# Three paired attention steps and one seven-product set in a fused attention and MLP kernel

## The chip, the core and the metric

The kernel runs on one core of one Trainium2 chip. Its engines are TensorE (PE, matmuls; PEld is its weight load), VectorE (DVE), ScalarE (ACT), GpSimd (POOL) and SyncE (SP, which here only issues DMAs; its queue is SPq). The metric is the device time of one execution in microseconds, the median of several runs.

## The reference, cut to what matters

```
for b in range(12):                       # blocks of 64 tokens, 4 batches x 8 heads, head_dim 64
    intra = einsum(qb, kb) * Dmask        # Dmask[i, j] = lam ** (i - j) for j <= i
    intra = einsum(intra, vb)
    inter = einsum(qb * lam_pow, kv_state)
    out[block] = intra + inter
    kv_state = lam_block * kv_state + einsum(kb * rev_pow, vb)
x = out as 3072 tokens x 512
h = x @ w_in                              # 512 x 2048: "first dense product"
result = gelu_tanh(h) @ w_out             # 2048 x 512: "second dense product"
```

All inputs and the result are float32; the kernel computes its products from float16 copies.

## The kernel before

**Steps.** The 3072 tokens are 12 superblocks of 256 tokens. A superblock has two halves of the heads, so there are 24 attention steps, numbered 0 to 23: step n is superblock n // 2, heads of half n % 2. A step loads q, k and v (`load_step`, line 70), casts and scales them (`prep_qk`: q on DVE at line 271, k on ACT at line 276; `prep_v`: v on POOL at line 258), and turns q and k around with a transposing DMA from step 9 on (line 280). `prep_v(s)` also issues the loads of step s + 3. Then come score matmuls of 64x64 blocks (`scores`, line 327), the causal mask on DVE into `PT` (`causal`, line 337, two instructions for a step), state products K (line 362), PT times v (line 376), and products with the carried state (line 385). `update` carries the state: t on DVE (lines 478 and 481), then u on POOL (line 488). ACT copies the step's output into `xT` (`x_out`, line 462). The first superblock of a batch has no carried state in its first half block, and the last one of a batch makes no state for a next.

**Two forms of a step.** `R(n, s)` runs the scores of step n and the outputs of the step s = n - 1. `burst(ns, ss)` does two steps of each at once, in whole classes: all scores, all PT products (line 411), all K products (line 425), all state products (line 436), then the masks. A burst holds four score banks, two O banks and two K banks of the eight PSUM banks of the pool `psM`, which every other matmul uses too. Before the change steps 8 to 17 go by `R` in the loop over `FILL`, and 18 to 23 by bursts.

**Dense products.** The tokens go through the dense products in seven groups: `groups = [[0, 1], [2], [3], [4, 5], [6, 7], [8, 9], [10, 11]]`. Group g becomes available when its last superblock's output is computed; `queue_group(g)` then appends its pieces to the list `filler`, and `fill(n)` runs the next n pieces between the parts of the attention steps. TensorE runs instructions in the order in which they are written, so the places of `fill` in the program are the schedule. In groups 3 and 4 (512 tokens) the first dense product is 16 pieces `mm1` of four matmuls of 128x512 (line 529), each followed by a gelu on ACT (line 533); the second is seven block products (`product`, line 606) in place of eight, with sums of blocks made on DVE (`sum_g`, line 576). Groups 5 and 6 (`SEVEN`) do the first product by seven block products as well: `seven(m, k)` (line 698) for m of 1 to 7 and sets k of 0 to 3, each four matmuls of 128x256. The sums of blocks of x are made by `sum_x` (line 677), those of w_in by `sum_win` (line 151). In a set, products 1, 6, 7 and 4 accumulate in one bank X one after the other: m1 is copied out by ACT (line 709), X after m6 is copied out by DVE (line 711), X after m7 is added to q by DVE (line 719), X after m4 goes through the gelu (line 715). 5 and then 3 share a bank Y, and 2 has a bank W. In groups 5 and 6 other pieces lie between these, and the sets alternate between two X banks.

**Buffers that the change touches.** Each transposing DMA writes one of four `qkT` buffers (pool `qkp`), which is free once the last product of its step has read it. The converted q, k and v have five buffers each, `PT` three, `u` four for each half. Every DMA in this part is issued by SP, in program order.

Of the kernel before, what the change touches and what calls it, by code (L numbers as in the profile page):

```python
# [9 lines left out]
FP16 = mybir.dt.float16  # L10
AF = mybir.ActivationFunctionType
ALU = mybir.AluOpType
# [3 lines left out]
def kernel(  # L16
# [10 lines left out]
    nc = tc.nc  # L27
    pin = tc.keep_in_program_order
    P = 128
    B, H, S, D = q.shape  # L30
    SB = 256
    NSB = S // SB
    HH = H // 2
# [136 lines left out]
    def load_ahead(s):  # L170
        if s < NSTEP:
            load_step(s)
# [72 lines left out]
    def prep(s):  # L245
        prep_qk(s)
        prep_v(s)

    def wide(t):
        return t.rearrange("p j h d -> p h j d")  # L250

    def decay(t, s):
        hs = halves[s % 2]
        return t[:, hs, :].unsqueeze(3).to_broadcast([P, HH, 2, D])

    def prep_v(s):
        tv = a16p.tile([P, 2, HH, D], FP16, tag="v16", name=f"v16_{s}")
        pin(nc.gpsimd.tensor_tensor(wide(tv[:]), ld32[s][2][:], decay(dv, s), ALU.mult))  # L258
        a16[s] = a16[s] + (tv,)
        if s >= 6:  # L260
            if s + 3 == FIRST_DMA_T + 1:
                load_step(s + 3, "qk")
            else:
                load_ahead(s + 3)

    def prep_qk(s):
        q32, k32, _ = ld32[s]
        tqk = a16p.tile([P, 2, 2, HH, D], FP16, tag="qk16", name=f"qk16_{s}")
        tq, tk = tqk[:, 0], tqk[:, 1]
        q_eng = nc.gpsimd if s == 3 else nc.vector  # L270
        pin(q_eng.tensor_tensor(wide(tq), q32[:], decay(dq, s), ALU.mult))  # L271
        if s == 0:
            inverse(halves[0])
            odd(halves[1])
            inverse(halves[1])
        pin(nc.scalar.activation(out=wide(tk), in_=k32[:], func=AF.Copy))  # L276
        a16[s] = (tq, tk)
        if s >= FIRST_DMA_T:
            o = qkp.tile([P, 2, 2, 2, P], FP16, tag="qkT", name=f"qkT_{s}")
            pin(nc.sync.dma_start_transpose(out=o[:].rearrange("p a j h t -> p (a j h) t"),  # L280
                                            in_=tqk[:].rearrange("p a j h d -> p (a j h d)")))
            qkT[s] = o
            if s == FIRST_DMA_T:
                load_step(s + 1, "v")
# [107 lines left out]
    def burst(ns, ss, *mix):  # L392


        for n in ns:
            scores(n)
        O = [ps_M.tile([P, 2, 2, P], FP32, tag="M", name=f"O{c}") for c in range(2)]
        seen = set()

        def start(kind, c, hl):  # L400
            new = (kind, c, hl) not in seen
            seen.add((kind, c, hl))
            return new

        qTs = [qkT.pop(s) for s in ss]
        for i, s in enumerate(ss):
            PT, tv = PTs.pop(s), a16.pop(s)[2]
            for hp in range(2):
                for jk in range(2):
                    for c, hl in TILES:  # L410
                        pin(nc.tensor.matmul(
                            O[c][half64(hl), i, hp, :], tv[half64(c), jk, 2 * hp + hl, :],
                            PT[half64(c), hl, hp, jk, :], start=start("O", c, hl), stop=False,
                            skip_group_check=True))
        if ns:
            K = [ps_M.tile([P, 2, P], FP32, tag="M", name=f"K{c}") for c in range(2)]
        for i, n in enumerate(ns):
            _, tk, tv = a16[n]
            last = (n // 2) % NSB == NSB - 1
            for jk in range(2):  # L420
                for hp in range(2):
                    for c, hl in TILES:
                        if c == 1 and last:
                            continue
                        pin(nc.tensor.matmul(
                            K[c][half64(hl), i, hp * D : hp * D + D],
                            tk[half64(c), jk, 2 * hp + hl, :], tv[half64(c), jk, 2 * hp + hl, :],
                            start=start("K", c, hl), stop=(jk == 1), skip_group_check=True))
            Kps[n] = [t[:, i] for t in K]
        for i, s in enumerate(ss):  # L430
            for c in range(2):
                if c == 0 and (s // 2) % NSB == 0:
                    continue
                u = us.pop((s, 0) if c else (s - 2, 1))
                for hp in range(2):
                    pin(nc.tensor.matmul(O[c][:, i, hp, :], u[:, hp].rearrange("p l d -> p (l d)"),
                                         qTs[i][:, 0, :, hp, half64(c)], start=False, stop=True,
                                         skip_group_check=True))
        for n in ns:
            causal(n)  # L440
        for i, s in enumerate(ss):
            x_out(s, [t[:, i].rearrange("p h t -> p (h t)") for t in O])
        sbg = ss[-1] // 2
        g, i = group_of[sbg]
        if i == len(groups[g]) - 1:
            queue_group(g, *mix)
        for n in ns:
            update(n, 0)
# [55 lines left out]
        return gs_kept[1:]  # L504

    SEVEN = (5, 6)
    SLOTS = {5: {1: 0, 2: 1, 5: 1, 6: 1, 3: 1, 7: 1}, 4: {1: 0, 2: 1, 5: 0, 6: 1, 3: 1, 7: 1}}
    groups = [[0, 1], [2], [3], [4, 5], [6, 7], [8, 9], [10, 11]]
    group_of = {sb: (g, i) for g, sbs in enumerate(groups) for i, sb in enumerate(sbs)}
# [2 lines left out]
    def queue_group(g, lead=0, per_set=0):  # L512
# [69 lines left out]
        def product(m, p, part=None):  # L582
# [42 lines left out]
            def store(T, ps=slice(0, NP), es=slice(0, 2)):  # L625
                r = row0 + T * HN
                rows = out[r : r + HN, :].rearrange("(p q) (e d) -> q p e d", q=P, e=2)
                whole = g == 3 or (g, T) == (4, 0)
                for i in [ps] if whole else [slice(i, i + 1) for i in range(ps.start, ps.stop)]:
                    pin(nc.sync.dma_start(out=rows[:, i, es], in_=out_tile(T)[:, i, es, :]))  # L630

# [53 lines left out]
        def seven(m, k):  # L685
# [48 lines left out]
                added(1, 1, "q")  # L734
            elif m == 4:
                pending.insert(0, lambda: gelu(1, 0, dst[:]))
            if k == HF // 2 - 1 and m in (3, 7, 4):
                release()

        def merge(lead, per_set):  # L740
# [71 lines left out]
        def behind(k, i0, i1, ms):  # L812

            piece = filler[at + k]

            def both():
                piece()
                sum_g(i0, i1, ms)

            filler[at + k] = both  # L820
# [3 lines left out]
        if g in SEVEN:  # L824
# [6 lines left out]
            for k, m in enumerate((2, 4, 3)):  # L831
                behind(len(parts) * k, 4, 8, (m,))
            return
        for i in range(HF):
            for fs in ([[i, i + HF]] if per == 2 else [[i], [i + HF]]):
                filler.append(lambda fs=fs: mm1(fs))
        for m, p in order:
# [4 lines left out]
        if per == 2:  # L842
            behind(5, 0, 4, (1, 2))
            behind(6, 0, 4, (4, 3))
            behind(7, 4, 8, (1,))
            behind(8, 4, 8, (2,))
            behind(9, 4, 8, (4,))
            behind(10, 4, 8, (3,))
        else:
            behind(9, 0, 4, (1, 2, 4, 3))  # L850
            w = 2 if g + 1 in SEVEN else 1
            for k, m in zip((0, 3, 7, 11) if w == 2 else (0, 1, 2, 4), (1, 2, 4, 3)):
                behind(n1 + k, 4, 8, (m,))

    def fill(n):
        for _ in range(min(n, len(filler))):
            filler.pop(0)()

    def R(n, s, ahead=None):

        if n is not None:
            scores(n)
        if ahead:
            ahead()
        products(n, s)
        if n is not None:
            causal(n)
        if s is not None and s % 2 == 1:
            g, i = group_of[s // 2]
            if i == len(groups[g]) - 1 and g > 0:  # L870
                queue_group(g)
        if n is not None:
            update(n, 0)

    def U(n):
        update(n, 1)
# [63 lines left out]
    for m in W_SUMS:  # L940
# [29 lines left out]
    prep_v(9)  # L970
    fill(2)

    FILL = {8: (0, 2, 1, 2), 9: (2, 2, 1, 2), 10: (0, 1, 1, 3), 11: (0, 2, 1, 2), 12: (0, 2, 1, 3),
            13: (0, 2, 1, 3), 14: (0, 3, 1, 3), 15: (0, 2, 1, 3), 16: (0, 2, 1, 3), 17: (0, 3, 1, 3)}
    for n, (a, b, c, d) in FILL.items():
        stage_t(n)
        fill(a)
        prep_qk(n + 2) if n == 8 else prep(n + 2)
        fill(b)
        R(n, n - 1)  # L980
        fill(c)
        U(n)
        if n == 8:
            prep_v(n + 2)
        if n == 17:
            prep_qk(20)
            fill(1)
            prep_qk(21)
            fill(1)
            prep_v(20)  # L990
            prep_v(21)
            fill(1)
        else:
            fill(d)
        if 8 < n < 17:
            sum_win((n - 7) // 2, (n - 1) % 2, nc.vector)

    burst((18, 19), (17,))
    fill(2)
    U(18)  # L1000
    U(19)
    fill(4)
    prep_qk(22)
    fill(2)
    burst((20, 21), (18, 19), 11, 4)
# [43 lines left out]
```

## Time and profile before

| | |
|---|---|
| Median of 8 runs | 199.88 us (199.78 to 201.21) |
| The profiled execution, its own time | 199.9 us |
| Its span, first to last instruction | 198.1 us |
| PE busy | 191.6 us (97%) |
| DVE busy | 152.2 us (77%) |
| ACT busy | 123.0 us (62%) |
| POOL busy | 73.4 us (37%) |
| Granted TensorE clock | 1.000 |

A line of the timeline gives start, duration (both in microseconds), engine, source line, operation, output<-inputs, shape and count; a bracket at its end is the idle time before it and what ended it. Line 462 or L462 is a line of the kernel before. Instructions of the same kind are merged into one line, so its duration runs from the first start to the last end. Neighbouring matmuls overlap in such a line, since their ends are modelled; what a stretch of matmuls costs is the distance from its start to the start of the next stretch.

### The profile page before, as it was taken

The numbers are of one execution on the slowest core, as the hardware profiler recorded it, in microseconds if no ns is written. First come the engines' busy times: TensorE is split into PE (matmuls) and PEld (weight loads), VectorE is DVE, ScalarE is ACT, GpSimd is POOL, SyncE is SP. The second block draws the span as 40 slices with busy tenths as digits, with TensorE's granted clock in tenths as the row PEclk, the third lists the DMA queues.
The fourth block names the chain that finished last, engine by engine and source line by source line (L and its number), as shares of the span: only waits on it lengthen the run. The fifth ranks groups of instructions, "written<-read, shape, count | busy, mean of one in ns | idle before, by whom it ended". The sixth has DMA issues, their size and how long they took to land.

```text
span 198.1 us, 5936 instructions
## 1 busy us (share of the span) xinstructions
PE 191.6 (97%) x2437; PEld 139.8 (71%) x2439; DVE 152.2 (77%) x296; ACT 123.0 (62%) x251; POOL 73.4 (37%) x85
## 2 busy tenths in 40 slices
PE   8879999999999999999999999999999999999993
PEld 2547544456888888744588755578888888888883
DVE  4988623689999989949899378998778997588720
ACT  3673978366694674577735486754668835778321
POOL 6594123357557652435433565047002030002000
PEclk9999999999999999999999999999999999999999
DMA  6999999999999999897964999520211300030205
GB/s 171 291 325 387 386 383 386 295 285 303 329 264 265 218 313 221 211 313 173 236 145 105 271 233 225 147 56 0 53 38 71 105 9 0 0 107 2 106 3 212
DMA packets 61706, 37.86 MB, mean 191 GB/s; under 512 B 17520, under 2 KB 54640, under 8 KB 61680
## 3 DMA queue, kind: packets, MB, share of 16 engines
q1 hardware_dynamic: 61136, 37.23, 72.7%
q8 instruction: 19, 0.31, 0.7%
q10 hardware_dynamic: 544, 0.26, 0.5%
q14 instruction: 7, 0.06, 0.1%
HBM read 27.26 MB, written 6.29 MB: 169 GB/s over the span
## 4 chain that ended last, share of the span: by engine, by line
PE 78%; DMA 12%; SPq 6%; ACT 1%; issue 1%; DVE 1%
PE Hps L529 21%; PE MX L606 17%; PE MY L606 9%; PE HX L698 7%; DMA wi<-in_moe_w_in_dram 7%; DMA k<-in_k_dram 5%; PE MW L606 4%; SPq L70 4%; PE HY L698 4%; PE S L327 3%; PE O2ps L544 3%; PE OK L385 2%; PE HW L698 2%; PE OK L376 2%; SPq L94 2%; PE Tps L298 1%
## 5 line engine op out<-in xcount | busy, mean ns | idle before, releaser
L529 PE MATMUL Hps<-xT,w_in 128*128 128x512 f16 (+1 forms) x288 | 51.0, 332 | 0.0
L488 POOL TENSOR_TENSOR u<-t,lumask 128x256 f16<-128x256 f32 x40 | 30.0, 763 | 49.4 <-DVE t L481 33.9
L529 PEld LDWEIGHTS <-w_in 128*128 128x128 f16 x288 | 27.7, 98 | 18.9
L533 ACT ACTIVATE gT<-Hps 128x512 f16<-128x512 f32 x56 | 33.0, 599 | 10.5 <-PE Hps L529 10.1
L337 DVE TENSOR_TENSOR PT<-S,mask 128x512 f16<-128x512 f32 x48 | 30.5, 682 | 7.5 <-PE S L327 7.3
L606 PEld LDWEIGHTS <-gs 128*128 128x128 f16 x320 | 31.3, 98 | 3.6
L258 POOL TENSOR_TENSOR v<-v,dv 128x512 f16<-128x512 f32 x24 | 29.7, 1241 | 7.0 <-DMA v<-in_v_dram 6.3
L606 PEld LDWEIGHTS <-gT 128*128 128x128 f16 x240 | 23.2, 98 | 3.5 <-ACT gT L533 0.5
L606 PE MATMUL MX<-w_sum,gs 128*128 128x256 f16 x160 | 21.4, 273 | 0.0
L271 DVE TENSOR_TENSOR qk<-q,dq 128x512 f16<-128x512 f32 x23 | 18.9, 824 | 1.1 <-DMA q<-in_q_dram 0.9
L276 ACT ACTIVATE qk<-k 128x512 f16<-128x512 f32 x24 | 15.0, 627 | 6.9 <-DMA k<-in_k_dram 6.9
L576 DVE TENSOR_TENSOR gs<-gT 128x1024 f16<-128x1024 f16 (+1 forms) x24 | 18.0, 755 | 1.6 <-ACT gT L533 1.5
L651 POOL TENSOR_TENSOR o<-u,q 128x512 f32<-128x512 f32 (+1 forms) x5 | 5.3, 1054 | 37.4 <-ACT u L623 37.4
L462 ACT ACTIVATE xT<-OK 128x256 f16<-128x256 f32 x34 | 13.0, 454 | 6.4 <-PE OK L385 6.1
L544 PE MATMUL O2ps<-w_out,gT 128*128 128x512 f16 x64 | 14.6, 379 | 0.0
L698 PEld LDWEIGHTS <-ws 128*128 128x128 f16 x128 | 12.5, 98 | 1.8
L623 ACT ACTIVATE u<-MX 128x256 f32<-128x256 f32 x18 | 6.9, 384 | 10.1 <-PE MX L606 10.1
L481 DVE SCALAR_TENSOR_TENSOR t<-t,lamu,OK 128x64 f32<-128x64 f32 x48 | 11.1, 274 | 1.3 <-issue 0.4
L327 PEld LDWEIGHTS <-qkT 64*64 64x64 f16 x384 | 6.0, 106 | 7.1 <-issue 3.6
L544 PEld LDWEIGHTS <-gT 128*128 128x128 f16 x64 | 6.1, 98 | 6.6
L606 PE MATMUL MY<-w_out,gs 128*128 128x256 f16 x80 | 10.7, 273 | 0.0
L606 PE MATMUL MX<-w_sum,gT 128*128 128x256 f16 x80 | 10.4, 273 | 0.0
(95 smaller groups left out, 311.8 us busy)
## 6 DMA issues: line engine op xcount, KB each, us to landing
q<-in_q_dram SPq DMA_DIRECT2D x24, 256.0 KB, 5.2
k<-in_k_dram SPq DMA_DIRECT2D x24, 256.0 KB, 5.2
v<-in_v_dram SPq DMA_DIRECT2D x23, 256.0 KB, 5.4
out_dram<-o SPq DMA_DIRECT2D x17, 256.0 KB, 4.1
wo<-in_moe_w_out_dram SPq DMA_DIRECT2D x4, 1024.0 KB, 9.7
wi<-in_moe_w_in_dram SPq DMA_DIRECT2D x4, 512.0 KB, 7.6
wi<-in_moe_w_in_dram SPq DMA_DIRECT2D x2, 1024.0 KB, 12.3
out_dram<-o SPq DMA_DIRECT2D x3, 512.0 KB, 5.1
```

Source lines behind the costliest of these rows:

```text
L258: pin(nc.gpsimd.tensor_tensor(wide(tv[:]), ld32[s][2][:], decay(dv, s), ALU.mult))
L271: pin(q_eng.tensor_tensor(wide(tq), q32[:], decay(dq, s), ALU.mult))
L276: pin(nc.scalar.activation(out=wide(tk), in_=k32[:], func=AF.Copy))
L337: pin(nc.vector.tensor_tensor(t[:, hl].rearrange("p b c d -> p b (c d)"), Sps[:].rearrange("p b c d -> p b (c d)"), mask[:].unsqueeze(1).t ...
L462: pin(nc.scalar.activation(out=d, in_=o, func=AF.Copy))
L488: pin(nc.gpsimd.tensor_tensor(u[:], state[half][:].unsqueeze(2).to_broadcast([P, 2, 2, D]), lumask[:, 2 * half : 2 * half + 2, :].unsqueez ...
L529: pin(nc.tensor.matmul(by_block(Hps[:, i, :]), w_in16[:, c, f * P : (f + 1) * P], x(c), start=(c == 0), stop=(c == NC - 1)))
L533: pin(nc.scalar.activation(out=dst, in_=Hps[:], func=AF.Gelu_apprx_tanh))
L544: pin(nc.tensor.matmul(O2[tau][0][:], gT[:, f % HF, f // HF, tau * P : (tau + 1) * P], w_out16[:, f, :], start=(n == 0), stop=(n == NF - 1)))
L576: pin(nc.vector.tensor_tensor(g_rows(m, i), g_rows(a, i), g_rows(b, i), op))
L606: pin(nc.tensor.matmul(dst, lhsT, rhs, start=(opens and i == 0), stop=(closes and i == HF - 1), skip_group_check=True))
L698: pin(nc.tensor.matmul(dst[:, i, :], w_in_block(a, slice(c, c + 1), slice(f * P, f * P + P))[:, 0], x_block(b, slice(c, c + 1))[:, 0], sta ...
```

## The change

It does three things. Steps 13 to 17 leave the loop and run as `burst((13, 14), (12,))`, `burst((15, 16), (13, 14))` and `R(17, 15)`, and the burst of 18 and 19 takes the outputs of 16 and 17. `prep_qk` and `prep_v` are split, so that the casts of steps 15 to 17 (`cast_qk`, `scale_v`) stand ahead of the preceding batch and the transposing DMAs of 16 and 17 (`transpose_dma`) behind it; loads, casts and `sum_win` move with them. The first set of group 4 (feature blocks 0, 1, 8 and 9) is computed by `seven`, in the order 1, plain, 2, 5, plain, 6, 3, plain, 7, 4, and the other twelve feature blocks stay plain pieces; `sum_xs[0](m)` makes the sums of x for it.

```diff
     def prep_v(s):
-        tv = a16p.tile([P, 2, HH, D], FP16, tag="v16", name=f"v16_{s}")
-        pin(nc.gpsimd.tensor_tensor(wide(tv[:]), ld32[s][2][:], decay(dv, s), ALU.mult))
-        a16[s] = a16[s] + (tv,)
+        scale_v(s)
         if s >= 6:
             if s + 3 == FIRST_DMA_T + 1:
                 load_step(s + 3, "qk")
             else:
                 load_ahead(s + 3)
 
+    def scale_v(s):
+        tv = a16p.tile([P, 2, HH, D], FP16, tag="v16", name=f"v16_{s}")
+        pin(nc.gpsimd.tensor_tensor(wide(tv[:]), ld32[s][2][:], decay(dv, s), ALU.mult))
+        a16[s] = a16[s] + (tv,)
+
     def prep_qk(s):
+        cast_qk(s)
+        transpose_dma(s)
+
+    def cast_qk(s):
...
         a16[s] = (tq, tk)
+        whole_qk[s] = tqk
+
+    whole_qk = {}
+
+    def transpose_dma(s):
+        tqk = whole_qk.pop(s)
         if s >= FIRST_DMA_T:
...
-        if i == len(groups[g]) - 1:
+        if ss[-1] % 2 == 1 and i == len(groups[g]) - 1:
             queue_group(g, *mix)
...
+    MIXED = 4
+    sum_xs = []
...
-                whole = g == 3 or (g, T) == (4, 0)
+                whole = g == 3
...
-            if k == HF // 2 - 1 and m in (3, 7, 4):
+            if (k == HF // 2 - 1 or g == MIXED) and m in (3, 7, 4):
                 release()
...
-        for i in range(HF):
+        if g == MIXED:
+            sum_xs.append(sum_x)
+            plain = [[f] for i in range(2, HF) for f in (i, i + HF)]
+            for m in (1, 0, 2, 5, 0, 6, 3, 0, 7, 4):
+                filler.append((lambda m=m: seven(m, 0)) if m else (lambda fs=plain.pop(0): mm1(fs)))
+            for fs in plain:
+                filler.append(lambda fs=fs: mm1(fs))
+        for i in range(HF) if g != MIXED else ():
...
-            behind(9, 0, 4, (1, 2, 4, 3))
+            n1 += 3 * (g == MIXED)
+            behind(n1 - 7, 0, 4, (1, 2) if g == 3 else (1, 2, 4, 3))
+            if g == 3:
+                behind(12, 0, 4, (4, 3))
...
-    FILL = {8: (0, 2, 1, 2), 9: (2, 2, 1, 2), 10: (0, 1, 1, 3), 11: (0, 2, 1, 2), 12: (0, 2, 1, 3),
-            13: (0, 2, 1, 3), 14: (0, 3, 1, 3), 15: (0, 2, 1, 3), 16: (0, 2, 1, 3), 17: (0, 3, 1, 3)}
+    FILL = {8: (0, 2, 1, 2), 9: (2, 2, 1, 2), 10: (0, 1, 1, 3), 11: (0, 2, 1, 2), 12: (0, 2, 1, 3)}
     for n, (a, b, c, d) in FILL.items():
         stage_t(n)
         fill(a)
-        prep_qk(n + 2) if n == 8 else prep(n + 2)
+        prep_qk(n + 2)
+        if n == 11:
+            scale_v(13)
+            load_step(16, "qk")
+        elif n > 8:
+            if n == 12:
+                load_step(16, "v")
+            prep_v(n + 2)
         fill(b)
         R(n, n - 1)
         fill(c)
         U(n)
         if n == 8:
             prep_v(n + 2)
-        if n == 17:
-            prep_qk(20)
-            fill(1)
-            prep_qk(21)
-            fill(1)
-            prep_v(20)
-            prep_v(21)
-            fill(1)
-        else:
-            fill(d)
-        if 8 < n < 17:
+        if n == 12:
+            prep_qk(15)
+            scale_v(15)
+        fill(d)
+        if n > 8:
             sum_win((n - 7) // 2, (n - 1) % 2, nc.vector)
 
-    burst((18, 19), (17,))
+    cast_qk(16)
+    scale_v(16)
+    fill(3)
+    burst((13, 14), (12,))
+    transpose_dma(16)
+    fill(1)
+    U(13)
+    U(14)
+    load_ahead(18)
+    load_ahead(19)
+    fill(2)
+    cast_qk(17)
+    scale_v(17)
+    fill(3)
+    burst((15, 16), (13, 14))
+    transpose_dma(17)
+    load_ahead(20)
+    fill(1)
+    U(15)
+    U(16)
+    fill(8)
+    prep(18)
+    R(17, 15)
+    fill(1)
+    U(17)
+    fill(1)
+    sum_win(3, 0, nc.vector)
+    fill(2)
+    prep(19)
+    sum_win(3, 1, nc.vector)
+    fill(2)
+    sum_win(4, 0, nc.vector)
+    fill(2)
+    sum_win(4, 1, nc.vector)
+    for m in (1, 2, 3, 4):
+        sum_xs[0](m)
+    prep_qk(20)
+    fill(3)
+    prep_qk(21)
+    fill(8)
+
+    burst((18, 19), (16, 17))
+    prep_v(20)
     fill(2)
     U(18)
     U(19)
-    fill(4)
+    prep_v(21)
+    fill(2)
     prep_qk(22)
     fill(2)
     burst((20, 21), (18, 19), 11, 4)
```

## The prediction

> **What bounds the kernel now.** I read the page first. TensorE is busy nearly all the time, and the chain that ended last is mostly TensorE:
>
> ```profile
> PE 191.6 (97%) x2437; PEld 139.8 (71%) x2439; DVE 152.2 (77%) x296; ACT 123.0 (62%) x251; POOL 73.4 (37%) x85
> ...
> PE 78%; DMA 12%; SPq 6%; ACT 1%; issue 1%; DVE 1%
> ```
>
> From 81 us to the end the list of waits has none for a matmul. So time changes only if TensorE gets less to do, or has to wait where it never waited. The stretch touched runs from the end of the step at 80.83 us to the burst at 126.36 us. TensorE's timeline there, first a single step, then a burst of one and of two output steps:
>
> ```profile
> 87.05 0.42 PE L327 MATMUL S<-qkT 64*64 64x128 f16 x16
> 87.30 0.29 PE L362 MATMUL OK<-v,qk 64*64 64x64 f16 x16
> 87.42 0.40 PE L376 MATMUL OK<-PT,v 64*64 64x128 f16 x16
> 87.75 0.28 PE L385 MATMUL OK<-qkT,u 128*128 128x128 f16 x2
> 87.87 6.21 PE L529 MATMUL Hps<-xT,w_in 128*128 128x512 f16 x28
> ...
> 117.99 0.64 PE L327 MATMUL S<-qkT 64*64 64x128 f16 x32
> 118.46 0.39 PE L411 MATMUL O<-PT,v 64*64 64x128 f16 x16
> 118.69 0.50 PE L425 MATMUL K<-v,qk 64*64 64x64 f16 x32
> 119.12 0.40 PE L436 MATMUL O<-qkT,u 128*128 128x128 f16 x4
> 119.36 7.07 PE L529 MATMUL Hps<-xT,w_in 128*128 128x512 f16 x32
> 126.36 0.64 PE L327 MATMUL S<-qkT 64*64 64x128 f16 x32
> 126.83 0.62 PE L411 MATMUL O<-PT,v 64*64 64x128 f16 x32
> 127.27 0.45 PE L425 MATMUL K<-v,qk 64*64 64x64 f16 x32
> 127.65 0.40 PE L436 MATMUL O<-qkT,u 128*128 128x128 f16 x4
> 127.89 2.75 PE L529 MATMUL Hps<-xT,w_in 128*128 128x512 f16 x12
> ```
>
> From start to start: 28 matmuls of 512 columns from 87.87 should end at 93.92, the next step begins at 94.01. So about 0.09 us goes at every change from wide matmuls to 64x64 ones. A single step costs 0.91 us with two state products (0.09 + 87.87 - 87.05), and 1.03 us with four. The bursts cost 1.45 and 1.62 us.
>
> The third view is what follows product 7 of a seven-product set, on TensorE and on DVE:
>
> ```profile
> 153.33 0.60 PE L698 MATMUL HX<-xs,ws 128*128 128x256 f16 x4
> 153.77 1.04 PE L606 MATMUL MX<-w_sum,gT 128*128 128x256 f16 x8
> 154.71 0.27 PE L698 MATMUL HX<-xs,w_in 128*128 128x256 f16 x1
> ```
>
> ```profile
> 153.97 0.69 DVE L719 TENSOR_TENSOR q<-HX,q 128x512 f32<-128x512 f32 x1
> ```
>
> Product 7 stops issuing at 153.77; DVE starts to read its bank X 0.20 us later and takes 0.69 us, to 154.66; product 4, which adds into the same bank, starts at 154.71. Nominally it was due at 153.77 + 8 x 0.109 = 154.64. Eight other matmuls only just cover a latency of 0.94 us.
>
> Last, SP's and POOL's timelines around the old burst of 18 and 19:
>
> ```profile
> 116.65 2.83 SPq L280 DMA_TRANSPOSE qkT<-qk  x1
> ...
> 119.64 2.22 SPq L280 DMA_TRANSPOSE qkT<-qk  x1
> ```
>
> ```profile
> 116.68 2.49 POOL L258 TENSOR_TENSOR v<-v,dv 128x512 f16<-128x512 f32 x2
> 121.22 2.78 POOL L488 TENSOR_TENSOR u<-t,lumask 128x256 f16<-128x256 f32 x4 [2.04 <-DVE t L478]
> ```
>
> The transposes of 20 and 21 are issued at 116.65 and 119.64, the second only when the burst has read step 17's qkT; they take 6.4 and 5.8 us to land, for scores wanted at 126.4 and 126.6. Across the program the transposes land 3.1 to 6.6 us after issue, median 5.4; with the DMA queues quiet I find 3.1, 3.2, 3.4, 4.0 and 4.9.
>
> **What the Trainium skill says.** "TensorE: Matmul & The Clock Gate", section "Wait — 56ns, not 53.3ns?": warm matmuls start N / 2.4 ns plus about 2.5 ns apart. The trace agrees: 0.216 us for 512 columns (6.91 us for 32 in the chain), 0.109 for 256 (1.75 for 16). "TensorEngine Tiling (Array Packing)", "Key Properties": changing the tiling mode drains the engine; the trace shows the 0.09 us above. "PSUM — Partial Sum Buffer", "Engine vs sequencer instructions": matmuls start and complete in program order. In the trace too nothing passes a waiting matmul, so a wait of product 4 holds everything behind it.
>
> **Part 1, the batches.** By blocks of the bursts above: entry 0.09, scores of two steps 0.47, PT products 0.23 for one step and 0.44 for two, K of two steps 0.40 (between 0.38 and 0.43), state products 0.06 each. (13,14),(12): 0.09 + 0.47 + 0.23 + 0.40 + 0.12 = 1.31, I take 1.35, as the old one-output burst had the dearer K. (15,16),(13,14), with a quarter of K absent and six state products: 0.09 + 0.47 + 0.44 + 0.33 + 0.36 = 1.69. R(17,15): 1.03. (18,19),(16,17), eight state products: 0.09 + 0.47 + 0.44 + 0.38 + 0.48 = 1.86. New sum 5.93 us. Old: two singles of 0.91, three of 1.03 and 1.45, 6.36 us. **Saved 0.43 us.**
>
> **Part 2, one set by seven.** Removed: 16 matmuls of 512 columns, 16 x 0.216 = 3.46 us. Added: 28 of 256, 28 x 0.109 = 3.06. **Saved 0.40 us.** Check of the ledger: one old product piece 0.87, 16 x 0.864, 14 x 0.873, 13 x 0.864 and the 6.36 us give 44.5 us, just the distance from 81.77 to 126.27. So TensorE had no hidden stalls to give back; 0.83 us is the whole prize.
>
> **Part 3, product 4 behind product 7.** The pieces consumed before the burst (18,19) are 41: one of group 2, 30 of group 3, ten of group 4. The last two are products 7 and 4, with nothing between. Only one set is done this way, so there is no second X bank to alternate with. Here nothing covers the 0.94 us. Queued behind: product 4, then the whole burst. **Lost 0.94 us**, sure to about 0.1. The other reuses are covered: m1's copy by 2.6 us of matmuls, q's copy by 1.30 (ACT needs 0.2 + 0.6, and at most one other 0.6), X's copy after m6 by 1.30 against 0.94.
>
> **Part 4, DVE.** Added: four x sums at 0.34 to 0.74 (taken 0.45), one copy and three additions at 0.69, 4.6 us. The old stretch from 81.4 to 118.5 had 7.9 us of DVE idle. Of the 3.3 left, the order spends about 2.2 ahead of the first burst's masks and 0.8 behind a late PE product. Walking the queue I get X's copy at its earliest, 0.2 us behind product 6, with about 1 us of slack. Slow forms (q casts of 1.09 beside POOL's 1.49, one `sum_win` of 1.53) can use it up: 0 to 0.7 us, taken as 0. For these pairs "SBUF — State Buffer", "Who interferes with whom", says that a DVE instruction with two SBUF inputs contends with a POOL one that reads SBUF; the trace's q cast of 0.68 alone and 1.09 beside v agrees.
>
> **Part 5, transposes.** Step 16's is issued when burst (13,14) ends, call it t, plus 0.1; its scores are wanted at t + 6 x 0.864 + 0.09 + 0.22 = t + 5.5. The queues are quiet, so it lands at t + 3.2 to t + 6; taken as free, bound 0.5. Step 17's has nine pieces: free. Steps 20 and 21 both wait, with four buffers held by 16 to 19, for burst (18,19) to read the qkT of 16 and 17. Before, only 21's did, and had eight pieces (6.91 us) of cover; now it has six. With t that burst's end: 20's issues at t, 1.24 us on SP; then the stalled store of group 3's second half, 0.45 to 0.94; 21's at t + 1.8. It lands 3.1 (quiet) to 6.4 later, the 512 KB store ahead of it in the queues. I take 4.5: t + 6.3 against t + 5.5 wanted, **0.8 us lost**, bounds 0 and 2.5. `prep_v(20)` and `prep_v(21)` now stand behind u of the burst on POOL: u(18,0), u(19,0), v20, u, u, v21 from t + 1.5, four times 0.65 and twice 1.25, v21 ready at t + 6.6. K of 21 wants it at t + 6.4 plus the stall before: hidden behind 0.8, and 0.2 us if the transpose is on time. Behind a late burst TensorE's whole tail waits; the masks' banks and the later sums shift with it.
>
> **Free edits.** The split store (two issues of 0.45 us on SP), the loads of 16 to 20 (each lands over 5 us ahead of its cast) and the moved casts lie on idle queues.
>
> **The sum.** 199.9 (the profiled execution; the median shown is 199.88) - 0.43 - 0.40 + 0.94 + 0.8 = **200.8 us**.
>
> **The rivals.** *The transposes keep up* (quiet landing of 3.1 us, v21 in time): 199.9 - 0.83 + 0.94 = 200.0, no change. For it: the pair stands alone on the queues. *The saving survives*: the order in the last slots covers product 4, or DVE's read is not what it waits for, and the transposes land: 199.1, faster. It is one mechanism, the wait at X; it decides below 0.3 us of stall. Against it: 154.66 and 154.71 above. *DVE becomes the bound* from 107 us on: with 0.7 us at product 7, 0.5 at step 16 and the 2.5 us transpose, up to 203.
>
> **How the numbers follow.** 0.3% of this kernel is 0.6 us, about what its measurement can tell from no change. Forecast 0.45 (slower), transposes keep up 0.30 (same), saving survives 0.12 (faster), DVE bound 0.13 (slower). Slower 0.58, same 0.30, faster 0.12. The range leaves out the faster case and the far end of the last: 199.6 to 202.0.
>
> **What would show it.** A 0.9 us hole on TensorE between products 7 and 4 of group 4, ended by DVE; a second hole in the scores of 21, ended by SP's transpose of 21; bursts of 1.3, 1.7 and 1.9 us. The prediction is wrong if product 4 follows within 0.1 us, if 21's transpose lands within 3.7 us of issue, or if holes appear at products 6, 3 or 7.

## The result, and the profile after

| | before | after |
|---|---|---|
| Median | 199.89 us (31 runs, 199.68 to 201.34) | 202.23 us (11 runs, 201.91 to 203.88) |
| Profiled execution, its own time | 199.90 us | 202.31 us |
| Its span | 198.1 us | 200.5 us |

The ratio is 1.012, with a 95% interval of 1.010 to 1.0141: slower. The forecast was +0.9 us with 202.0 as its upper end; it came to +2.3 us, and the median lies above that end.

The page after, engines and chain:

```profile
PE 192.0 (96%) x2449; PEld 141.3 (70%) x2451; DVE 160.1 (80%) x304; ACT 124.0 (62%) x253; POOL 75.5 (38%) x85
...
PE 72%; DMA 12%; SPq 6%; DVE 5%; issue 1%; ACT 1%
```

DVE's share of the chain was 1% and is 5%: TensorE now waits for DVE. The list of TensorE's waits has three behind step 12, where before had none, and its timeline (after) shows where they are. Below, **C** is the start of the scores of burst (18,19), **D** that of burst (20,21), and **H** the first wide matmul behind D (line 544 after, 529 before):

```profile
117.72 0.60 PE L713 MATMUL HX<-xs,ws 128*128 128x256 f16 x4
119.10 0.60 PE L713 MATMUL HX<-xs,w_in 128*128 128x256 f16 x4 [0.78 <-DVE q L734]
119.62 0.64 PE L340 MATMUL S<-qkT 64*64 64x128 f16 x32
...
126.63 0.42 PE L340 MATMUL S<-qkT 64*64 64x128 f16 x16
127.90 0.42 PE L340 MATMUL S<-qkT 64*64 64x128 f16 x16 [0.85 <-DMA qkT<-qk]
...
128.59 0.76 PE L438 MATMUL K<-v,qk 64*64 64x64 f16 x32
129.28 0.40 PE L449 MATMUL O<-qkT,u 128*128 128x128 f16 x4
130.18 2.75 PE L544 MATMUL Hps<-xT,w_in 128*128 128x512 f16 x12 [0.50 <-DVE PT L350]
```

The first hole stands between products 7 and 4: product 4 was due at 117.72 + 4 x 0.109 = 118.16 and starts at 119.10, 0.94 late. Behind D three waits come one after another. The second half of the scores (step 21, its transposing DMA) is 1.03 late: due at 126.63 + 0.24. K takes 0.69 us in place of 0.38 (v of 21 on POOL). H starts 0.90 behind the state products in place of 0.24. Together D to H takes 3.55 us, where before took 1.53 (126.36 to 127.89).

DVE's timeline from C's masks to D's masks, before and then after:

```profile
118.45 2.48 DVE L337 TENSOR_TENSOR PT<-S,mask 128x512 f16<-128x512 f32 x4 [1.19 <-PE S L327]
...
122.78 0.74 DVE L576 TENSOR_TENSOR gs<-gT 128x1024 f16<-128x1024 f16 x1 [0.68 <-ACT gT L533]
123.56 0.98 DVE L576 TENSOR_TENSOR gs<-gs,gT 128x1024 f16<-128x1024 f16 x1
...
125.78 0.68 DVE L271 TENSOR_TENSOR qk<-q,dq 128x512 f16<-128x512 f32 x1
126.82 2.48 DVE L337 TENSOR_TENSOR PT<-S,mask 128x512 f16<-128x512 f32 x4 [0.35 <-PE S L327]
```

```profile
120.09 2.48 DVE L350 TENSOR_TENSOR PT<-S,mask 128x512 f16<-128x512 f32 x4 [1.04 <-PE S L340]
...
123.65 0.93 DVE L591 TENSOR_TENSOR gs<-gT 128x1024 f16<-128x1024 f16 x1
124.62 1.41 DVE L591 TENSOR_TENSOR gs<-gs,gT 128x1024 f16<-128x1024 f16 x1
...
128.00 1.53 DVE L278 TENSOR_TENSOR qk<-q,dq 128x512 f16<-128x512 f32 x1
129.45 2.47 DVE L350 TENSOR_TENSOR PT<-S,mask 128x512 f16<-128x512 f32 x4
```

From masks to masks (the start of C's first mask to the start of D's first) it was 8.37 us with 1.03 us idle; it is 9.36 with none. The same four sums and one cast took 3.69 us of DVE and take 5.80. In the old stretch POOL ran only u; now v of 20 and 21 stand in it, and two of the u's come later, behind v of 20 (POOL's timeline, after):

```profile
123.99 1.49 POOL L266 TENSOR_TENSOR v<-v,dv 128x512 f16<-128x512 f32 x1
...
127.48 1.49 POOL L266 TENSOR_TENSOR v<-v,dv 128x512 f16<-128x512 f32 x1
```

D's masks begin 2.82 us behind its scores (0.46 before), and H comes 0.73 us behind the first mask: with four score banks, two O and two K banks taken, the next wide matmul needs a bank that a mask sets free.

The span in segments, from TensorE's timeline of each profiled execution. S12 is the start of step 12's scores; the last column is from the start of ACT's last copy to the end of the span:

| kernel | S12 at | S12 to C | C to D | D to H | H to last copy | rest |
|---|---|---|---|---|---|---|
| before | 80.83 | 37.16 | 8.37 | 1.53 | 67.27 | 2.94 |
| after | 81.02 | 38.60 | 7.01 | 3.55 | 67.26 | 3.06 |

S12 to D is 45.53 and 45.61; C itself stands two pieces later in the new order, so that the first two columns compare only as a sum. S12's own time moved between 80.5 and 82.1 us over the runs below, so small differences are read from segments.

### The profile page after: what moved, and what is told of

It reads as the page before. It is cut to its first block, busy times and chain, and to the rows that moved or that the text cites. A ratio compares the mean times of both kernels' runs of the same rounds, so it can differ in the third digit from the quotient of the medians.

```text
span 200.5 us, 5968 instructions
## 1 busy us (share of the span) xinstructions
PE 192.0 (96%) x2449; PEld 141.3 (70%) x2451; DVE 160.1 (80%) x304; ACT 124.0 (62%) x253; POOL 75.5 (38%) x85
## 4 chain that ended last, share of the span: by engine, by line
PE 72%; DMA 12%; SPq 6%; DVE 5%; issue 1%; ACT 1%
PE MX L621 17%; PE Hps L544 16%; PE MY L621 9%; PE HX L713 8%; DMA wi<-in_moe_w_in_dram 7%; DMA k<-in_k_dram 5%; PE MW L621 4%; SPq L70 4%; PE HY L713 4%; PE O2ps L559 3%; PE S L340 3%; PE HW L713 2%; DVE gs L591 2%; DVE PT L350 2%; SPq L94 1%
## 5 line engine op out<-in xcount | busy, mean ns | idle before, releaser
L544 PE MATMUL Hps<-xT,w_in 128*128 128x512 f16 (+1 forms) x272 | 47.7, 329 | 0.5 <-DVE PT L350 0.5
L544 PEld LDWEIGHTS <-w_in 128*128 128x128 f16 x272 | 26.3, 98 | 17.4 <-issue 0.6
L548 ACT ACTIVATE gT<-Hps 128x512 f16<-128x512 f32 x52 | 30.7, 598 | 8.7 <-PE Hps L544 8.2
L266 POOL TENSOR_TENSOR v<-v,dv 128x512 f16<-128x512 f32 x24 | 30.8, 1288 | 7.1 <-DMA v<-in_v_dram 4.4
L621 PEld LDWEIGHTS <-gT 128*128 128x128 f16 x240 | 23.2, 98 | 3.6 <-ACT gT L548 0.5
L713 PEld LDWEIGHTS <-ws 128*128 128x128 f16 x144 | 14.0, 98 | 2.4
L475 ACT ACTIVATE xT<-OK 128x256 f16<-128x256 f32 x26 | 10.0, 455 | 7.5 <-PE OK L398 7.4
L475 ACT ACTIVATE xT<-O 128x256 f16<-128x256 f32 x22 | 8.0, 459 | 7.2 <-PE O L449 5.5
L713 PEld LDWEIGHTS <-w_in 128*128 128x128 f16 x108 | 10.5, 98 | 2.5 <-issue 1.0
L340 PE MATMUL S<-qkT 64*64 64x128 f16 x384 | 9.2, 221 | 1.7 <-DMA qkT<-qk 0.9
L713 PE MATMUL HX<-xs,ws 128*128 128x256 f16 x72 | 10.8, 273 | 0.0
```

What stands on the lines that cost most here:

```text
L340: pin(nc.tensor.matmul(Sps[hl][half64(c), hp, jk, :], o[half64(hl), 1, jk, hp, half64(c)], o[half64(hl), 0, :, hp, half64(c)], start=True, ...
L475: pin(nc.scalar.activation(out=d, in_=o, func=AF.Copy))
L544: pin(nc.tensor.matmul(by_block(Hps[:, i, :]), w_in16[:, c, f * P : (f + 1) * P], x(c), start=(c == 0), stop=(c == NC - 1)))
L548: pin(nc.scalar.activation(out=dst, in_=Hps[:], func=AF.Gelu_apprx_tanh))
L621: pin(nc.tensor.matmul(dst, lhsT, rhs, start=(opens and i == 0), stop=(closes and i == HF - 1), skip_group_check=True))
L713: pin(nc.tensor.matmul(dst[:, i, :], w_in_block(a, slice(c, c + 1), slice(f * P, f * P + P))[:, 0], x_block(b, slice(c, c + 1))[:, 0], sta ...
```

## The experiments

**Theories.** *Transpose* (the one on record): the second half of D's scores waits for its transposing DMA, and the rest only shifts with it. *DVE*: D's masks come late by DVE's own queue, slowed by POOL's v; H then follows DVE whatever the scores do. *Product 4*: the 0.94 us hole reaches the end in full. All edits are to the kernel after, unless said otherwise; the times of before given with them were 199.87 to 199.96 us in each group.

**A fifth `qkT` buffer.** To make room, the buffer `rel` shares one with `m1`.

```diff
-    qkp = ctx.enter_context(tc.tile_pool(name="qkp", bufs=4))
+    qkp = ctx.enter_context(tc.tile_pool(name="qkp", bufs=5))
-    rel = const.tile([P, 2, 2, 64], FP32)
+    rel = mtp.tile([P, 2, 2, 64], FP32, tag="m1", name="rel")
```

> The changed kernel with five qkT buffers in place of four (paid for by placing the start-up tile rel in another pool), so that the transposes of 20 and 21 are issued earlier and land in time. If the masks that POOL's work makes late set the end of the burst (20,21), its scores start on time but the wide matmul behind it still waits for DVE until about 3.5 us after the burst's start: 202.0 to 202.3 us. If the late transpose sets it, 1.0 us or more comes back: 201.2 us or less.

Measured: 204.28 us, 1.0214 (1.0181 to 1.0247). TensorE's timeline from D:

```profile
126.81 0.64 PE L340 MATMUL S<-qkT 64*64 64x128 f16 x32
...
129.21 0.32 PE L438 MATMUL K<-v,qk 64*64 64x64 f16 x16 [1.19 <-POOL v L266]
...
130.36 2.88 PE L544 MATMUL Hps<-xT,w_in 128*128 128x512 f16 x8 [0.50 <-DVE PT L350]
```

The wait for the transpose is gone, K waits for v instead, and D to H is 3.55 us as before the edit. So the transpose theory falls: its wait was real, and its removal was worth nothing. (K's wait, which took its place, goes as well in the run with three repairs below.) The time is outside both forecasts. Of the 2.6 us by which the profiled execution is longer than that of the kernel after, 1.7 lie behind H, in a lower clock (last section), 0.6 ahead of C, where step 16's scores waited 0.38 us for their transpose, and 0.8 behind the last copy (S12 itself came 0.4 us earlier).

**v of 20 and 21 scaled ahead of burst (18,19)**, into a pool of six.

```diff
+    v16p = ctx.enter_context(tc.tile_pool(name="v16", bufs=6))
-        tv = a16p.tile([P, 2, HH, D], FP16, tag="v16", name=f"v16_{s}")
+        tv = v16p.tile([P, 2, HH, D], FP16, tag="v16", name=f"v16_{s}")
...
+    scale_v(20)
+    scale_v(21)
     fill(8)
 
     burst((18, 19), (16, 17))
-    prep_v(20)
+    load_ahead(23)
...
-    prep_v(21)
```

> The changed kernel with v of 20 and 21 scaled on POOL ahead of the burst (18,19), as before the change, with a sixth v buffer. If POOL beside DVE makes the masks late, DVE's four sums of group 4 take 0.7 to 1.0 us each again, K and the masks wait no longer, and only the transpose's 1.0 us stays: 201.2 us. If the transposes alone matter, nothing changes: 202.1 to 202.3 us.

Measured: 202.74 us, 1.0132 (1.011 to 1.0155). The sums and the cast on DVE fall back to old sizes:

```profile
126.41 0.98 DVE L592 TENSOR_TENSOR gs<-gs,gT 128x1024 f16<-128x1024 f16 x1
...
128.94 0.68 DVE L279 TENSOR_TENSOR qk<-q,dq 128x512 f16<-128x512 f32 x1
```

The four sums and the cast take 4.10 us in place of 5.80: moving the v's gives back 1.70 of the 2.11 us, and the rest goes with u, which stands beside three of the sums here. Masks to masks is 7.66 us, and D to H 2.57, with only the transpose's wait left. But POOL now runs v beside the sums of x, where DVE had no room either. They take up to 1.38 us each, and the q casts behind them come late. ACT's copy of q (line 725) goes into one of the buffers of the loaded q, and begins 0.1 us after a cast ends; product 3 waits for it:

```profile
118.22 0.60 PE L714 MATMUL HY<-xT,ws 128*128 128x256 f16 x4 [0.77 <-ACT q L725]
```

S12 to C grows from 38.60 to 39.96 us. What was won at D was lost ahead of C, and both forecasts were missed.

**The cast of q of step 22 behind burst (20,21).**

```diff
-    prep_qk(22)
     fill(2)
     burst((20, 21), (18, 19), 11, 4)
+    prep_qk(22)
     fill(3)
```

> The changed kernel with the cast of step 22 behind the burst (20,21) and no longer ahead of its masks on DVE. If DVE's queue sets the end of the burst, the masks start some 1.4 us sooner and the wait behind the burst (0.7 us) goes, K's wait for v21 stays: 201.6 us. If it is the transposes: 202.2 us.

Measured: 201.34 us, 1.0077 (1.0059 to 1.0095). One DVE instruction less between the masks, masks to masks 7.91 us, and D to H is 2.87: 0.68 us less at H and 0.9 us less in the median, with the transpose's wait still there (1.09). That is what the DVE theory has.

**A plain piece between products 7 and 4.**

```diff
-            for m in (1, 0, 2, 5, 0, 6, 3, 0, 7, 4):
+            for m in (1, 2, 5, 0, 6, 3, 0, 7, 0, 4):
```

> The changed kernel with the set's order 1, 2, 5, plain, 6, 3, plain, 7, plain, 4: a plain piece now lies between products 7 and 4. If the hole there costs what it shows, 0.7 to 0.9 us come back: 201.4 us. If what follows is bound by something else and swallows it, 202.0 to 202.3 us.

Measured: 201.61 us, 1.0084 (1.0065 to 1.0103). Product 4 (118.34) starts 0.94 us behind the start of the plain piece (117.40), against 0.87 with no wait. The hole is gone as forecast, and the median falls by 0.62 us. S12 to C falls by 0.57 and not by 0.94: products 3 and 4 start 0.13 and 0.07 us late and the scores of step 16 cost 0.16 more. C to H is 10.55 us, as in the kernel after (10.56), though K now waits for a gelu and D starts 0.48 us later: H follows C's masks, not D.

**These together**: the fifth buffer, v of 21 right behind v of 20, and the q cast of 22 behind D; then the same with the new order of products.

```diff
     burst((18, 19), (16, 17))
     prep_v(20)
+    prep_v(21)
     fill(2)
     U(18)
     U(19)
-    prep_v(21)
     fill(2)
-    prep_qk(22)
     fill(2)
     burst((20, 21), (18, 19), 11, 4)
+    prep_qk(22)
     fill(3)
```

> The changed kernel with three repairs of the burst (20,21) at once: five qkT buffers (with rel in another pool), v of 21 scaled ahead of the second u's on POOL, and the cast of step 22 behind the burst on DVE. The hole between products 7 and 4 stays. If the transpose, K's wait for v and the late masks are the whole of the burst's 2.0 us, they all go: 200.2 us. If something else holds the burst, 200.8 us or more.

> The same three repairs and the set's order 1, 2, 5, plain, 6, 3, plain, 7, plain, 4 as well. If the saved TensorE time of 0.8 us is real and only hidden by these waits: 199.4 us, faster than the kernel before by 0.2%. If the saving is not real, 199.9 us or more.

Measured: 203.08 us, 1.0146 (1.0117 to 1.0174), and 201.92 us, 1.009 (1.0067 to 1.0114). Both missed. In the first, two lines of TensorE's timeline:

```profile
96.33 0.42 PE L340 MATMUL S<-qkT 64*64 64x128 f16 x16 [1.01 <-DMA qkT<-qk]
...
130.63 2.75 PE L544 MATMUL Hps<-xT,w_in 128*128 128x512 f16 x12 [0.83 <-DVE PT L350]
```

The v's still stand beside the sums, now both beside the same sums (two of 1.42 us), and masks to masks is 8.34 us. The mask is what H waits for. The waits for transpose and v are gone, and D to H falls to 2.52 us, by just what masks to masks fell. What D won, 1.0 us, was lost ahead of C: S12 to C is 39.81 us in place of 38.60, with the wait of 1.01 us in step 16's scores shown above. Further on a sum on DVE is 0.38 us late for its product (137.69). The end after the last copy is longer too (3.60 and 4.16 us; see the last section).

**The batches alone**, with no product of seven: plain pieces, five in place of eight ahead of C.

```diff
-    MIXED = 4
+    MIXED = None
...
-    for m in (1, 2, 3, 4):
-        sum_xs[0](m)
...
-    fill(8)
+    fill(5)
```

> The batches alone: group 4's first product all in plain pieces, five of them in place of eight pieces ahead of the burst (18,19). The ledger says 0.43 us less TensorE time. If the moved casts, v's and transposes hold the burst (20,21) by themselves, 199.9 - 0.4 + 2.0 = 201.5 us. If the seven-product set crowds that burst, no more than 200.0 us.

Measured: 202.19 us, 1.0101 (1.0076 to 1.0126). Its profiled execution reached S12 1.2 us later than before's. From S12 to H it takes 48.61 us, before 47.06: +1.55, which is a saving of 0.47 up to D (45.06 in place of 45.53) and a loss of 2.02 at D. The forecast of 201.5 lies just inside the interval, which reaches from 201.5 to 202.5 us. D to H is 3.55 us, the same as in the kernel after, with another split (1.36 for the transpose, 0.29 for the mask). So the batches alone make the whole loss at D.

**The seven-product set alone**, in the schedule of before, with the code for the set as in the change: ten pieces ahead of C, and v of 20 and 21 still scaled ahead of C.

```diff
...
+            for m in (1, 2, 3, 4):
+                sum_xs[0](m)
...
-            prep_v(20)
+            prep_v(20, False)
...
-            fill(1)
+            fill(6)
...
+    load_ahead(23)
...
-    fill(4)
+    fill(2)
```

> The seven-product set alone, in the schedule before: the set's ten pieces stand ahead of the burst (18,19), six pieces behind it, and the loads of step 23 behind that burst. TensorE saves 0.40 us and loses 0.94 between products 7 and 4: 200.4 us. If the added work on DVE makes the masks late too, up to 201.4 us. If the hole does not show outside the batches, 199.5 us.

Measured: 205.73 us, 1.0267 (1.0227 to 1.0308), a miss. Product 3 waits 2.48 us for ACT's copy of q, which waits for the cast of q on DVE, which stands behind the sums of x, two of them 1.26 us long beside POOL. Then the clock falls to half (last section). But D to H is 1.54 us and masks to masks 7.66: where the v's do not stand behind C, D's masks are in time. C to D took 0.7 us more than in the kernel after (7.71 us), with its first half at the lower clock. At full clock DVE would have been about 0.3 us late, an estimate by the rule further down (8.85 against 8.54). This run gives no clean price for the set.

**Two more pieces between C and D**, so eight as before; then the same with the new order of products.

```diff
     prep_qk(22)
-    fill(2)
+    fill(4)
     burst((20, 21), (18, 19), 11, 4)
```

> The changed kernel with eight pieces in place of six between the bursts (18,19) and (20,21), taken from the three plain pieces behind the second. Nothing else is edited. If only cover ahead of that burst is missing, its 2.0 us go: 200.2 us. If DVE is behind over the whole stretch up to the sums of group 4, the masks no longer wait but the first products that read those sums do, and 1 to 1.6 us of the 2.0 come back as that wait: 201.2 to 201.9 us.

> The same eight pieces, and the set's order with a plain piece between products 7 and 4. 0.6 us less than the run with eight pieces alone: 199.6 us if only cover was missing, 200.6 to 201.3 us if DVE is behind.

Measured: 203.28 us, 1.0182 (1.0167 to 1.0197), and 202.35 us, 1.0134 (1.0118 to 1.0149). C to H of the first is again 10.55 us, with 1.73 us more of matmuls done in it. All of that was lost again further on:

```profile
135.13 1.05 PE L621 MATMUL MY<-w_sum,gs 128*128 128x256 f16 x8 [0.29 <-DVE gs L591]
...
140.82 0.60 PE L713 MATMUL HX<-xs,ws 128*128 128x256 f16 x4 [1.06 <-DVE u L726]
...
185.19 0.60 PE L713 MATMUL HX<-xs,w_in 128*128 128x256 f16 x4 [0.82 <-DVE q L734]
```

By the starts these are delays of 0.46 and 1.23 us: together 1.69, the lead of 1.73. DVE's copy of X stands at C + 20.74 us here and at C + 20.60 in the kernel after. TensorE may be early; it is held to DVE. The third (due at 184.20, 0.99 late) is a second product 4 directly behind a product 7, since the shift by two pieces took away the piece between them in a later set. With the new order in the first such set, it is 0.93 us less in the median; the profiled execution (203.17 us) shows no gain, as its step 16's scores waited 0.74 us, by the profile for a mask. Both forecasts were missed.

**Before, with `rel` sharing the buffer.** It tests whether that edit has a cost of its own.

```diff
-    rel = const.tile([P, 2, 2, 64], FP32)
+    rel = mtp.tile([P, 2, 2, 64], FP32, tag="m1", name="rel")
```

> The kernel before with the start-up tile rel in the other pool, as in the runs with five qkT buffers, whose last store landed 0.6 to 1.1 us later than in the others. If the moved addresses cause that, 200.5 to 200.9 us; if not, 199.9 us.

Measured: 199.84 us over 22 runs, 1.0007 (0.9997 to 1.0017): none.

**All of D's reasons at once**: six v buffers, v of 20 with v of 19, v of 21 three pieces later than its transpose, the transpose of 21 issued ahead of a store that stalls SP, and the new order of products.

```diff
-            for m in (1, 0, 2, 5, 0, 6, 3, 0, 7, 4):
+            for m in (1, 2, 5, 0, 6, 3, 0, 7, 0, 4):
...
-    prep(19)
+    prep_qk(19)
+    scale_v(19)
+    scale_v(20)
+    load_ahead(22)
...
-    fill(3)
     prep_qk(21)
+    fill(3)
+    scale_v(21)
     fill(8)
 
     burst((18, 19), (16, 17))
-    prep_v(20)
+    load_ahead(23)
     fill(2)
     U(18)
     U(19)
-    prep_v(21)
```

> The changed kernel with v of 20 and 21 scaled ahead of the burst (18,19) as early as their loads allow (sixth v buffer), the transpose of 21 ahead of the stalled store on SP, and a plain piece between products 7 and 4. If DVE slowed by POOL, the transpose and the hole are all that the change loses, a remainder of 0.3 us at the burst is left: 199.7 us. If DVE is too full without POOL beside it as well, 200.3 us or more.

Measured: 201.86 us, 1.0103 (1.0085 to 1.0121). At D nothing is late any more: D to H 1.53 us, masks to masks 7.65, with C to D at 7.49 us. But ahead of C:

```profile
116.33 0.60 PE L714 MATMUL HY<-xT,ws 128*128 128x256 f16 x4 [1.13 <-ACT q L725]
```

Product 3 was due at 114.60 + 0.44 = 115.04, so it is 1.29 us late: again the casts of q on DVE came late behind sums of x slowed by POOL (up to 1.49 us). K waits 0.27 us for a gelu's bank. S12 to H is 48.05 us, 1.0 above before. The forecast's second case, 200.3 us or more, is what came. No version of the changed kernel beat the kernel before.

**C to H by one rule.** If DVE sets H, then C to H is 0.46 (scores to first mask) + masks to masks on DVE + 0.73 (first mask to H), in us:

| kernel | masks to masks | rule | C to H | ended by |
|---|---|---|---|---|
| after | 9.36 | 10.55 | 10.56 | mask |
| fifth `qkT` buffer | 9.36 | 10.55 | 10.55 | mask |
| new order | 9.36 | 10.55 | 10.55 | mask |
| batches alone | 9.36 | 10.55 | 10.55 | mask |
| two more pieces | 9.35 | 10.54 | 10.55 | mask |
| together | 8.34 | 9.53 | 9.53 | mask |
| together, new order | 8.33 | 9.52 | 9.52 | mask |
| q of 22 later | 7.91 | 9.10 | 9.88 | transpose |
| v ahead | 7.66 | 8.85 | 9.57 | transpose |
| all of D's reasons | 7.65 | 8.84 | 9.02 | TensorE |
| two more pieces, new order | 9.35 | 10.54 | 10.74 | TensorE |

In seven kernels the sum comes out within 0.01 us, so that the 0.46 and the 0.73 stay the same, with different waits on TensorE ahead of the masks; and in no kernel of the table does the profile list idle time of DVE from masks to masks. In the last four DVE was done, and something else ended last. With the edits that shorten DVE's stretch alone (v ahead, q of 22 later), that shows what holds H in the kernel after.

## Why the prediction was wrong, step by step

- **The batches' saving, 0.43, and the set's, 0.40: right.** S12 to D is 0.08 us longer than before with a hole of 0.94 in it, so 0.86 us of matmuls went, against 0.83. The batches alone give 0.47 of it, which leaves 0.39 for the set. The bursts, each from start to start with 0.09 for the entry: 1.34 for (13,14),(12) against 1.35, 1.71 against 1.69, and 1.82 against 1.86.
- **Product 4 behind product 7, 0.94: right, at its place.** It is 0.94 us, ended by DVE's addition, and a piece between them removes it. As it delays C, and DVE's stretch up to D's masks starts at C, it passes on to H; with the piece between, 0.6 us came back.
- **"Step 16's ... taken as free, bound 0.5": right here, with little to spare.** No wait there in the kernel after; 0.38 and 1.01 us in two runs with five buffers, and 0.23 in the one with v ahead.
- **"0.8 us lost" at the transpose of 21: the failed step.** Its own term was nearly right. The transpose was issued 2.6 us behind the burst's end (forecast 1.8), as the one ahead of it took 1.82 us on SP and not 1.24; it landed 3.9 us later (forecast 4.5). The scores were 1.03 us late. But D cost 2.02 us, and the transpose was not what set that: without its wait H came no earlier. What failed is the clause that the masks' banks "shift with it". They have a timing of their own, DVE's queue from C, and it ran 2.0 us later than it would have needed to. C to H by TensorE alone is 7.01 + 1.53 = 8.54 us; DVE's rule gives 10.55, and with the sums and the cast at their old durations it would give 10.55 - 2.11 = 8.44 (an estimate).
- **"`prep_v(20)` and `prep_v(21)` ... hidden behind 0.8": wrong in kind.** I followed their cost on POOL's own queue (v of 21 late for K, put at nothing behind the transpose and at 0.2 without its wait: it was 0.31 and 1.19 us, as v of 21 was ready 7.6 us behind the burst and not 6.6) and not on DVE, beside which they run. They, and the u's behind them, took the four sums and the cast from 3.69 to 5.80 us; the run with the v's moved gives 1.70 of these 2.11 us to the v's. I had named the very effect in the prediction: "SBUF — State Buffer", section "Who interferes with whom", says that a DVE instruction with two SBUF inputs contends with a POOL instruction that reads SBUF. This case agrees (a cast of 0.68 us took 1.53, a sum of 0.98 took 1.41), and I applied it to the stretch ahead of C and not to that behind it, to which the change moves the v's.
- **"DVE ... 0 to 0.7 us, taken as 0": right ahead of C, wrong behind it.** I counted only the added 4.6 us. Behind C nothing is added, but the stretch is two pieces shorter (8.37 to 7.01 us from C to D) and its DVE work 2.1 us longer. DVE is busy for 9.85 of the 10 us from 120 and 9.82 of those from 130; before it was 8.90 and 9.25.
- **The rivals.** *DVE becomes the bound*, to which I gave 0.13, was what happened, though at another place than I put it; had *the transposes keep up* come true, D would have cost 2.0 us all the same, as the run with five buffers shows. The two holes and the three bursts that I named as signs came true, and the sum was still wrong: none of the signs looked at the masks.

With D's term at 2.02 in place of 0.8, the sum is 199.9 - 0.83 + 0.94 + 2.02 = 202.0 us; the profiled execution's 202.31 has 0.19 us more ahead of S12 and 0.12 more at the end.

## What to carry to other kernels

When an edit moves an elementwise instruction of GpSimd, price it also on VectorE's queue, in the new place: look up which two-input instructions will stand beside it, and take their slow durations. Where several waits end within a microsecond, find out by each one's own queue when it would end if the others were gone; the last of them is the cost, and removing any other is worth nothing. A microsecond saved on TensorE in a stretch that VectorE fills is only a longer wait later, as the run with two more pieces shows.

## What the runs showed that I had not expected

**A hole can cost twice.** In the profiled run with a fifth `qkT` buffer, TensorE had 1.19 and 0.50 us of waits within three microseconds, and then ran at half clock. Four windows of that kernel, of a microsecond each: behind the length stand the busy times of PE, PEld, DVE, ACT and POOL, then the granted clock, the DMA share and GB/s:

```profile
128.00:129.00 1.00, 0.02 (x4) 0.00 (x0) 1.00 (x2) 0.40 (x1) 1.00 (x1) 1.00 0.09 25
129.00:130.00 1.00, 0.65 (x20) 0.48 (x20) 1.00 (x2) 0.11 (x1) 0.16 (x1) 1.00 0.00 0
...
131.00:132.00 1.00, 1.00 (x4) 0.40 (x3) 1.00 (x2) 0.43 (x1) 0.00 (x0) 0.55 1.67 129
132.00:133.00 1.00, 1.00 (x3) 0.30 (x2) 1.00 (x6) 0.17 (x1) 0.38 (x1) 0.50 0.61 133
```

The clock is 0.50 in the next window too and 0.74 in that from 134: some 3.4 us at about half clock, and H to the last copy 68.95 us in place of 67.26. Three of that kernel's six runs have a mean clock of 0.989 to 0.991 and took 204.9 to 205.4 us; the other three have 0.996 or more and took 203.4 to 203.7. "TensorE: Matmul & The Clock Gate", "What's actually happening", tells of two clocks, a half and a full one, and of a window of about 3.4 us that decides; the half clock and its length agree. That section gives one idle window as the condition for the half clock; here TensorE was partly busy in every window of that length that one can lay over the holes. In the seven-product set alone it came after one hole of 2.48 us and held for about 6.8 us. The kernel after kept the full clock there in its profiled execution, with 1.35 us of waits spread over the same kind of stretch. What decides between them no run here settles.

**The end differs with the build.** From the start of ACT's last copy to the end of the span it is 2.94 us before and 3.06 after, but 3.60 to 4.16 in the three builds with five `qkT` buffers and 3.67 in the one with all of D's reasons at once; elsewhere it is 2.9 to 3.25. `rel`'s place alone leaves it at 2.97. The cause stays open.
